# Two-chunk score groups from chunk 10 on, and another order of the first third, in an RWKV-6 layer followed by a squared-ReLU network

## The chip, the core and the metric

The kernel runs on one core of a Trainium2 chip. The metric is device time in microseconds of that core, taken as the median over several executions. One further execution was profiled, and all views of a profile come from that one.

## What is computed

Two parts follow each other. The first is a linear-attention recurrence with a decay for every channel, over 4 batches, 8 heads, 768 steps and a head size of 48. The second is a two-layer network with a squared ReLU on the 3072 tokens of 8 x 48 = 384 features, with 2048 hidden units.

```python
for t in range(S):                       # for every batch and head; state is D x D
    cur = np.einsum('bhd,bhe->bhde', u[None] * kt, vt)
    y[:, :, t] = np.einsum('bhd,bhde->bhe', rt, state + cur)
    state = wt[:, :, :, None] * state + np.einsum('bhd,bhe->bhde', kt, vt)
...
h = x @ w_in          # x: (3072, 384), w_in: (384, 2048)
g = np.maximum(h, 0.0) ** 2
out = g @ w_out       # w_out: (2048, 384)
```

Inputs and outputs are float32. The kernel's matrix products take bfloat16.

## The kernel before

The recurrence is done in chunks of 128 steps: 6 chunks in each of 4 batches, numbered `s` = 0 to 23. Every chunk is a short chain of steps, and each step is a small function that one word of a long string names. For chunk `s` the words are:

- `ld:s:w`, `ld:s:r`, `ld:s:k`, `ld:s:v`: four loads of 192 KB, all issued on SyncE's queue, 192 bytes to a row. Seven buffers of each kind exist.
- `lw` (ScalarE): logarithm of the decay into one of `NLW` buffers. `cum` (TensorE): running sums over the chunk by a triangular matrix, into the two-bank accumulator `cp`; for early chunks (`s < V5`) a second matmul with the negative inclusive triangle; and, for all but a batch's last chunk, five small matmuls with the decay's total.
- `exp` (ScalarE): exponentials of the sums in place, and of the total into `a_c`. For `s >= V5` one sum serves both signs; then `rw` (ScalarE) and `kw` (GpSimd) multiply `k` by the inverse decay first.
- `rd` (VectorE): `r` and `k` times the exponentials. `tr` (TensorE) transposes both, `rkt` (VectorE) copies them out. `p` (TensorE): scores within the chunk, head pairs in halves of 64 rows, into `cp` again. `pm` (VectorE): the mask, from `cp`.
- `su` (TensorE), `ts` (VectorE), `sn` (GpSimd): the state for the next chunk. `ku`, `qp`, `vq` (GpSimd) and `q` (VectorE): the current step's own term with `u`. `v` (ScalarE): `v` in bfloat16.
- `y` (TensorE), `ysb` (VectorE), `yt` (TensorE), `xt` (ScalarE): the output of the chunk, transposed into `xT`.

The network works on blocks of two chunks, `i` = 0 to 11. `m1:i:g:b` is six matmuls of 256 columns into bank `b` of the four banks called `mm`; `rl` (ScalarE) evicts them with the ReLU, `gt` (VectorE) squares. `m2:i:mt:q:b` is four matmuls of 384 columns, a quarter `q` of the sum for one half block; `os` (ScalarE) evicts it and `store` writes it. The weights come as 8 blocks each, `ld:h:I` and `ld:h:O`, 384 KB, and are cast by `cast` on ScalarE or VectorE in turn: `m1` of group `g` needs block I of the same number, `m2` of quarter `q` needs blocks O 2q and 2q+1. `warm` is filler matmuls with no use for the result.

[...] `cp` has two, `y` one, `tr` one (used in turn by `tr`, `su` and `yt`), `mm` four. `cp`, `y`, `tr` and each `mm` bank have one buffer, so the next writer waits until the last reader is done.

The order of the work is written out by hand in the string `order`. Each engine, SyncE's queue included, gets its instructions in the order of the words, and nothing is re-ordered later:

```python
with tc.manual_schedule(engines={E.PE, E.DVE, E.Activation, E.Pool, E.SP}):
    for word in order.split():
        name, *args = word.split(":")
        run[name](*[int(x) if x.isdigit() else x for x in args])
```

## Time and profile before

| what | value |
|---|---|
| median of 6 runs | 199.31 us (198.58 to 200.25) |
| the profiled execution, its own time | 198.89 us |
| its span, first to last instruction | 197.1 us |
| TensorE matmul busy | 188.2 us |
| VectorE, ScalarE, GpSimd busy | 143.9, 131.5, 109.2 us |
| moved from and to memory | 25.17 MB, 4.72 MB |
| `p` on TensorE, 192 matmuls | 9.5 us |
| warm matmuls, 52 recorded | 16.2 us |
| granted TensorE clock | 1.00 |

A chain through all the work of a profile has one slowest engine in each stretch, and the share of a whole span hides which. The profile is therefore read by stages, and a line of the code stands as L with its number. The profiler's span is shorter than the time of the execution by 1.8 us, which lie before the first and after the last instruction.

### The profile page before, as it was taken

What the parts mean: (1) busy time and instruction counts of PE and PEld (TensorE: products, weight loads), DVE (VectorE), ACT (ScalarE), POOL (GpSimd) and SP (SyncE); (2) the same over time, 40 slices, a digit from 0 to 9 for tenths busy, and PEclk for the clock granted to TensorE, in tenths of its full rate; (3) what the DMA queues carried; (4) which work ended last, traced back from release to release, by engine and by line L of the source; (5) the groups of instructions that cost most, each with busy time, mean ns of one, the idle gap of its engine ahead of it and who ended that gap; (6) DMA issues with size and microseconds to landing.
All of it is one profiled execution on the core that took longest, in us unless ns stands there. A gap on an engine that the chain in (4) does not pass through costs nothing.

```text
span 197.1 us, 4956 instructions
## 1 busy us (share of the span) xinstructions
PE 188.2 (95%) x1954; PEld 136.0 (69%) x1958; DVE 143.9 (73%) x202; ACT 131.5 (67%) x278; POOL 109.2 (55%) x124
## 2 busy tenths in 40 slices
PE   7999959999999999999999999999999999999992
PEld 2355546776578777768777688877777778778650
DVE  3369966987788979987969876977897885844210
ACT  3625637895589887878975767678776668438221
POOL 6278643017589899793997299430999390010000
PEclk9999999999999999999999999999999999999999
DMA  6999789989989999899999078605730000015013
GB/s 129 196 212 222 254 233 291 326 216 267 209 177 200 201 203 224 196 196 200 233 200 202 3 171 230 147 16 130 167 68 0 3 0 2 3 40 203 0 40 120
DMA packets 108696, 30.20 MB, mean 153 GB/s; under 512 B 100481, under 2 KB 108674, under 8 KB 108674
## 3 DMA queue, kind: packets, MB, share of 16 engines
q1 hardware_dynamic: 108674, 29.89, 66.0%
q8 instruction: 15, 0.25, 0.5%
q14 instruction: 7, 0.06, 0.1%
HBM read 25.17 MB, written 4.72 MB: 152 GB/s over the span
## 4 chain that ended last, share of the span: by engine, by line
PE 63%; SPq 15%; DMA 8%; DVE 5%; POOL 4%; issue 2%; ACT 2%; DVEq 0%; POOLq 0%; ACTq 0%
PE mm L300 25%; PE mm L324 24%; SPq L67 9%; SPq L90 5%; PE tr L222 4%; DMA w_raw<-in_w_dram 3%; PE cp L234 3%; DMA v_raw<-in_v_dram 3%; DMA rk_raw<-in_r_dram 2%; PE y L269 2%; POOL ku L172 2%; DVE rdec_buf L213 1%; PE tr L285 1%; PE y L274 1%; PE cp L196 1%
## 5 line engine op out<-in xcount | busy, mean ns | idle before, releaser
L300 PE MATMUL mm<-xT,wi_sb 128*128 128x256 bf16 x576 | 72.7, 273 | 2.5 <-ACT wi_sb L104 2.0
L324 PE MATMUL mm<-wo_sb,gt 128*128 128x384 bf16 x384 | 71.6, 326 | 0.0
L309 ACT ACTIVATE rl<-mm 128x512 f16<-128x512 f32 x96 | 55.4, 598 | 18.9 <-PE mm L300 14.1
L300 PEld LDWEIGHTS <-wi_sb 128*128 128x128 bf16 x576 | 54.1, 98 | 12.3 <-ACT wi_sb L104 2.2
L324 PEld LDWEIGHTS <-gt 128*128 128x128 bf16 x384 | 35.8, 98 | 19.0
L317 DVE TENSOR_TENSOR gt<-rl 128x1024 bf16<-128x1024 f16 x48 | 40.2, 854 | 9.5 <-ACT rl L309 9.5
L261 POOL TENSOR_TENSOR S<-t_state,a_c 128x384 bf16<-128x384 f32 x20 | 17.7, 885 | 30.1 <-DVE t_state L257 16.4
L239 DVE TENSOR_TENSOR pmT<-cp,tri_strict 128x1024 bf16<-128x1024 f32 x24 | 29.3, 1219 | 4.3 <-PE cp L234 3.9
L184 POOL TENSOR_TENSOR vq<-v_raw,q 128x384 f32<-128x384 f32 x24 | 21.7, 906 | 17.1 <-DVE q L180 15.4
L172 POOL TENSOR_TENSOR ku<-rk_raw,u_bc 128x384 f32<-128x384 f32 x24 | 25.2, 1048 | 10.5 <-DMA rk_raw<-in_k_dram 5.9
L213 DVE TENSOR_TENSOR rdec_buf<-rk_raw,cp 128x768 bf16<-128x768 f32 x24 | 22.8, 950 | 10.1 <-ACT a_c L209 5.5
L176 POOL TENSOR_TENSOR qprod<-rk_raw,ku 128x384 f32<-128x384 f32 x24 | 25.6, 1074 | 0.6
L226 DVE COPY rkT<-tr 128x1024 bf16<-128x1024 bf16 x24 | 16.5, 687 | 8.4 <-PE tr L222 8.2
L164 POOL TENSOR_TENSOR rk_raw<-rk_raw,rw 128x384 f32<-128x384 f32 x16 | 18.6, 1165 | 5.2 <-ACT rw L160 5.1
L329 ACT ACTIVATE o_sb<-mm 128x384 f32<-128x384 f32 x24 | 11.6, 491 | 9.6 <-PE mm L324 9.5
L288 ACT COPY xT<-tr 128x384 bf16<-128x384 bf16 x24 | 11.5, 479 | 9.6 <-PE tr L285 9.3
L338 PE MATMUL mm<-warm 128*128 128x512 bf16 x52 | 16.2, 427 | 1.5 <-DVE ones L132 1.3
L279 DVE TENSOR_TENSOR y_sb<-vq,y 128x384 bf16<-128x384 f32 x24 | 13.2, 549 | 6.0 <-PE y L274 5.4
L156 ACT ACTIVATE lw_buf<-w_raw 128x384 bf16<-128x384 f32 x24 | 12.4, 521 | 6.3 <-DMA w_raw<-in_w_dram 6.3
L222 PE MATMUL tr<-ident,rdec_buf 128*128 128x128 bf16 x192 | 14.6, 219 | 0.4 <-DVE rdec_buf L213 0.3
L222 PEld LDWEIGHTS <-rdec_buf 128*128 128x128 bf16 x192 | 12.3, 98 | 2.9 <-DVE rdec_buf L213 1.2
L180 DVE TENSOR_REDUCE q<-qprod 128x8 f32<-128x384 f32 x24 | 13.0, 544 | 0.2 <-POOL qprod L176 0.2
(53 smaller groups left out, 178.4 us busy)
## 6 DMA issues: line engine op xcount, KB each, us to landing
w_raw<-in_w_dram SPq DMA_DIRECT2D x24, 192.0 KB, 3.8
rk_raw<-in_r_dram SPq DMA_DIRECT2D x24, 192.0 KB, 3.8
rk_raw<-in_k_dram SPq DMA_DIRECT2D x24, 192.0 KB, 3.9
v_raw<-in_v_dram SPq DMA_DIRECT2D x24, 192.0 KB, 3.8
out_dram<-o_sb SPq DMA_DIRECT2D x24, 192.0 KB, 2.2
...
u_row<-in_u_dram SPq DMA_DIRECT2D x1, 1.5 KB
```

The costliest lines, as they stand in the source:

```text
L67: nc.sync.dma_start(out=dst, in_=src[b, :, c * C:(c + 1) * C, :].rearrange("h c d -> c h d"))
L164: nc.gpsimd.tensor_mul(k_s, k_s, tiles.pop(("rw", s))[:])
L172: nc.gpsimd.tensor_mul(ku[:], raw["rk", s][:, 1], u_bc[:])
L176: nc.gpsimd.tensor_mul(qp[:], raw["rk", s][:, 0], tiles.pop(("ku", s))[:])
L184: nc.gpsimd.tensor_mul(vq[:], raw["v", s][:], tiles.pop(("q", s))[:, :, None].to_broadcast([C, H, D]))
L213: nc.vector.tensor_mul(rdec[:, :, :, 0:D], raw["rk", s][:], tiles.pop(("cs", s))[:, :, 0:DM].rearrange("p a (h d) -> p a h d", h=H))
L222: nc.tensor.transpose(ps_tr[:, i, p, :], rdec[:, i, 2 * p:2 * p + 2, :], ident[:])
L239: nc.vector.tensor_mul(pmT[:].rearrange("p e a t -> p (e a) t"), tiles.pop(("p", s))[:].rearrange("p e (a t) -> p (e a) t", a=HP), tri_str ...
L300: nc.tensor.matmul(ps1[:, j * width:(j + 1) * width], wi_sb[:, kk, n * 128:(n + 1) * 128], xT[:, kk, s0 * C:s0 * C + width], start=(kk == ...
L309: nc.scalar.activation(tiles["rl", i, q][:, j], tiles.pop(("m1", i, g))[:], AF.Relu, scale=RS)
L317: nc.vector.tensor_mul(tiles["gt", i][:, 4 * q:4 * q + 4, :].rearrange("p a b -> p (a b)"), rl, rl)
L324: nc.tensor.matmul(tiles["m2", i, mt][:, 0:DM], gt[:, n, mt * 128:(mt + 1) * 128], wo_sb[:, n, :], start=(n == 0), stop=(n == NT - 1))
```

## The change

Five things differ.

1. From chunk 10 on, `p:s:b0:b1` writes the scores of two chunks with one run of matmuls: chunk `s` into `cp` as before, chunk `s + 1` into two `mm` banks. The second chunk's mask is done by two `pmh`, one for each bank.
2. `V5` goes from 8 to 5, so chunks 5, 6 and 7 take the form with one running sum and get `rw` and `kw`. `NLW` goes from 3 to 4.
3. The five small decay matmuls move from `cum` to `su`, from a `cp` bank to the `tr` bank, and their exponential moves from `exp` to a word of its own, `ac`.
4. The last half block's second layer is done by `last`, in two halves of 192 columns, each with its own eviction (the first on ScalarE, the second on VectorE) and its own store.
5. The order string is another one throughout. In the first third, chunks 4 and 5 are loaded ahead of most weight blocks. `u` is loaded into row 0 of `u_bc`.

The diff, with the order string cut to its first part, the first two-chunk group and the end:

```diff
...
     u_bc = consts.tile([C, H, D], FP32)
-    u_row = consts.tile([1, H, D], FP32)
+    u_row = u_bc[0:1]
     ones_row = consts.tile([1, C], FP32)
     nc.vector.memset(ones_row[:], 1.0)
     def load_u():
-        nc.sync.dma_start(out=u_row[:], in_=u[None])
+        nc.sync.dma_start(out=u_row, in_=u[None])
     def ub_():
         ps = tiles["ub"] = ps_y_pool.tile([C, H, D], FP32, name="y")
-        nc.tensor.matmul(ps[:], ones_row[:], u_row[:], start=True, stop=True)
+        nc.tensor.matmul(ps[:], ones_row[:], u_row, start=True, stop=True)
     def uc_():
         nc.scalar.copy(u_bc[:], tiles.pop("ub")[:])
...
     nc.gpsimd.memset(other_head[:], 0.0)
     nc.gpsimd.memset(other_head[0:DP, :, 1:2], -30000.0)
     nc.gpsimd.memset(other_head[DP:C, :, 0:1], -30000.0)
-    V5 = 8
-    NLW = 3
+    V5 = 5
+    NLW = 4
     lw_bufs = []
     for i in range(NLW):
         t = consts.tile([C, H, DP], BF16, name=f"lw_buf{i}")
...
     def cum_(s):
         lw = tiles["lw", s]
         cs = tiles["cs", s] = ps_cp.tile([C, 2, 512], FP32, name="cp")
-        if s % NCH < NCH - 1:
-            nc.tensor.matmul(cs[:, 0, DM:DM + 2 * HP], ident[:], other_head[:], start=True,
-                             stop=False, skip_group_check=True)
-            for p in range(HP):
-                nc.tensor.matmul(cs[:, 0, DM + 2 * p:DM + 2 * p + 2], lw[:, 2 * p:2 * p + 2, :],
-                                 ones2[:], start=False, stop=True, skip_group_check=True)
         nc.tensor.matmul(cs[:, 0, 0:DM], tri_strict[:], lw[:, :, 0:D], start=True, stop=True)
         if s < V5:
             nc.tensor.matmul(cs[:, 1, 0:DM], tri_incl_neg[:], lw[:, :, 0:D], start=True, stop=True)
...
         else:
             nc.scalar.activation(cs[:, 1, 0:DM], cs[:, 0, 0:DM], AF.Exp, scale=-1.0)
             nc.scalar.activation(cs[:, 0, 0:DM], cs[:, 0, 0:DM], AF.Exp)
-        if s % NCH < NCH - 1:
-            a_c = tiles["a_c", s] = a_small.tile([C, HP, 2], FP32, name="a_c")
-            nc.scalar.activation(a_c[:], cs[:, 0, DM:DM + 2 * HP].rearrange("p (a e) -> p a e", e=2), AF.Exp)
+    def ac_(s):
+        a_c = tiles["a_c", s] = a_small.tile([C, HP, 2], FP32, name="a_c")
+        nc.scalar.activation(a_c[:], tiles["su", s][:, DM:DM + 2 * HP].rearrange("p (a e) -> p a e", e=2), AF.Exp)
     def rd_(s):
         rdec = tiles["rdec", s] = rdec_bufs[s % NRD]
...
         rkT = tiles["rkT", s] = a_mid.tile([C, 2, HP, C], BF16, name="rkT")
         nc.vector.tensor_copy(rkT[:], tiles.pop(("tr", s))[:])
-    def p_(s):
-        rkT = tiles["rkT", s]
-        ps_p = tiles["p", s] = ps_cp.tile([C, 2, 512], FP32, name="cp")
-        for p in range(HP):
+    def p_(s, *banks):
+        tiles["p", s] = ps_cp.tile([C, 2, 512], FP32, name="cp")
+        dst = {s: [tiles["p", s][:, e] for e in range(2)]}
+        if banks:
             for e in range(2):
-                rows = slice(e * DP, (e + 1) * DP)
-                nc.tensor.matmul(ps_p[:, e, p * C:(p + 1) * C], rkT[rows, 1, p, :],
-                                 rkT[rows, 0, p, :], start=True, stop=True)
+                tiles["ph", s + 1, e] = bank(banks[e])
+            dst[s + 1] = [tiles["ph", s + 1, e][:] for e in range(2)]
+        for i in dst:
+            rkT = tiles["rkT", i]
+            for p in range(HP):
+                for e in range(2):
+                    rows = slice(e * DP, (e + 1) * DP)
+                    nc.tensor.matmul(dst[i][e][:, p * C:(p + 1) * C], rkT[rows, 1, p, :],
+                                     rkT[rows, 0, p, :], start=True, stop=True)
     def pm_(s):
         pmT = tiles["pmT", s] = a_mid.tile([C, 2, HP, C], BF16, name="pmT")
...
             tiles.pop(("p", s))[:].rearrange("p e (a t) -> p (e a) t", a=HP),
             tri_strict[:, None, :].to_broadcast([C, 2 * HP, C]))
+    def pmh_(s, e):
+        if ("pmT", s) not in tiles:
+            tiles["pmT", s] = a_mid.tile([C, 2, HP, C], BF16, name="pmT")
+        nc.vector.tensor_mul(
+            tiles["pmT", s][:, e], tiles.pop(("ph", s, e))[:].rearrange("p (a t) -> p a t", a=HP),
+            tri_strict[:, None, :].to_broadcast([C, HP, C]))
+
     def su_(s):
-        rdec, v_bf = tiles["rdec", s], tiles["v", s]
-        ps_su = tiles["su", s] = ps_tr_pool.tile([C, HP, 2, D], FP32, name="tr")
+        rdec, v_bf, lw = tiles["rdec", s], tiles["v", s], tiles["lw", s]
+        ps_su = tiles["su", s] = ps_tr_pool.tile([C, 512], FP32, name="tr")
         for p in range(HP):
-            nc.tensor.matmul(ps_su[:, p], rdec[:, 1, 2 * p:2 * p + 2, :],
+            nc.tensor.matmul(ps_su[:, p * 2 * D:(p + 1) * 2 * D], rdec[:, 1, 2 * p:2 * p + 2, :],
                              v_bf[:, 2 * p:2 * p + 2, :], start=True, stop=True)
+        nc.tensor.matmul(ps_su[:, DM:DM + 2 * HP], ident[:], other_head[:], start=True,
+                         stop=False, skip_group_check=True)
+        for p in range(HP):
+            nc.tensor.matmul(ps_su[:, DM + 2 * p:DM + 2 * p + 2], lw[:, 2 * p:2 * p + 2, :],
+                             ones2[:], start=False, stop=True, skip_group_check=True)
     def ts_(s):
-        ps_su = tiles.pop(("su", s))
+        ps_su = tiles.pop(("su", s))[:, 0:DM].rearrange("p (a e d) -> p a e d", a=HP, e=2)
         ts = tiles["ts", s] = a_mid.tile([C, HP, 2, D], FP32, name="t_state")
         if s % NCH == 0:
-            nc.vector.tensor_copy(ts[:], ps_su[:])
+            nc.vector.tensor_copy(ts[:], ps_su)
         else:
-            nc.vector.tensor_add(ts[:], tiles["S", s][:], ps_su[:])
+            nc.vector.tensor_add(ts[:], tiles["S", s][:], ps_su)
     def sn_(s):
         S = tiles["S", s + 1] = a_mid.tile([C, HP, 2, D], BF16, name="S", bufs=3)
...
         t0 = (blocks[i][0] + mt) * C
         nc.sync.dma_start(out=out[t0:t0 + C, :], in_=tiles.pop(("o", i, mt))[:])
+    def last_(i, mt, b, j):
+        gt, cols = tiles["gt", i], slice(j * DM // 2, (j + 1) * DM // 2)
+        ps, o_sb = bank(b), o_pool.tile([C, DM], FP32, name="o_sb")
+        for n in range(NT):
+            nc.tensor.matmul(ps[:, 0:DM // 2], gt[:, n, mt * 128:(mt + 1) * 128], wo_sb[:, n, cols],
+                             start=(n == 0), stop=(n == NT - 1))
+        if j == 0:
+            nc.scalar.activation(o_sb[:, cols], ps[:, 0:DM // 2], AF.Copy, scale=1.0 / (RS * RS))
+        else:
+            nc.vector.tensor_scalar_mul(o_sb[:, cols], ps[:, 0:DM // 2], 1.0 / (RS * RS))
+        t0 = (blocks[i][0] + mt) * C
+        nc.sync.dma_start(out=out[t0:t0 + C, cols], in_=o_sb[:, cols])
+
     def warm_(n, b):
         ps = bank(b)
         for _ in range(n):
...
-    run = dict(rw=rw_, kw=kw_, lw=lw_, v=v_, cum=cum_, exp=exp_, rd=rd_, tr=tr_, rkt=rkt_, p=p_, pm=pm_, su=su_, ts=ts_,
+    run = dict(rw=rw_, kw=kw_, ac=ac_, last=last_, pmh=pmh_, lw=lw_, v=v_, cum=cum_, exp=exp_, rd=rd_, tr=tr_, rkt=rkt_, p=p_, pm=pm_, su=su_, ts=ts_,
...
-        ld:0:w ld:0:r warm:6:0 ld:1:w ld:0:k lw:0 ld:0:u cum:0 ld:0:v warm:4:1 ld:1:v lw:1 ld:1:r exp:0 ub ld:1:k rd:0
-        warm:1:2 uc ld:2:w cum:1 v:0 ku:0 exp:1 su:0 ld:3:w warm:3:3 ts:0 v:1 tr:0 sn:0 ld:2:v warm:9:0 rd:1 ku:1 ld:2:r
-        rkt:0 qp:0 lw:2 ld:2:k p:0 qp:1 tr:1 pm:0 ld:0:I warm:4:1 ld:3:r ld:4:w rkt:1 cum:2 y:0 exp:2 su:1 ld:3:k
-        warm:10:2 ts:1 v:2 q:1 sn:1 rd:2 ku:2 ld:3:v q:0 cast:i:0:0 p:1 su:2 vq:0 pm:1 warm:5:3 lw:3 ld:1:I ld:2:I qp:2
-        ld:3:I ts:2 cum:3 ld:4:I ysb:0 vq:1 tr:2 exp:3 ld:4:r y:1 rkt:2 ku:3 ld:4:v warm:1:0 rd:3 yt:0 warm:3:1 xt:0
-        qp:3 ysb:1 lw:4 tr:3 sn:2 v:3 p:2 rkt:3 warm:2:2 pm:2 yt:1 ld:5:I warm:4:3 xt:1 cast:i:0:1 cast:i:1:0 p:3 ld:6:I
-        y:2 q:2 m1:0:0:0 pm:3 vq:2 ld:4:k cast:i:2:0 m1:0:2:1 su:3 rl:0:0 ld:5:w ysb:2 m1:0:4:2 ts:3 v:4 cum:4 q:3
-        ld:7:I yt:2 rl:0:4 m1:0:1:3 vq:3 exp:4 y:3 ld:0:O sn:3 warm:3:0 ysb:3 ld:1:O xt:2 cast:i:1:1 rl:0:2 ld:2:O yt:3
-        warm:1:2 ld:3:O m1:0:3:0 xt:3 rd:4 ku:4 ld:6:w cast:i:2:1 m1:1:4:2 ld:4:O qp:4 rl:0:1 su:4 ld:5:k m1:1:5:1 lw:5
-        gt:0:0 m1:0:5:3 rl:0:3 ts:4 rl:1:4 m1:1:2:0 gt:0:1 rl:1:5 m1:1:0:2 cast:i:3:1 rl:0:5 tr:4 cast:i:3:0 rl:1:2
-        m1:1:3:1 rkt:4 ld:5:r cast:o:0:1 m1:0:6:3 gt:0:2 p:4 rl:1:3 m1:1:1:0 cast:o:1:0 rl:1:0 m1:1:6:1 pm:4 rl:1:1
-        ld:5:O m1:1:7:2 cast:o:0:0 ld:6:O gt:1:2 y:4 lw:6 ld:7:O m1:0:7:0 gt:1:0 rl:0:6 cum:5 gt:1:1 rl:0:7 ld:6:k
-        m2:0:0:0:3 exp:5 cast:o:1:1 m2:0:1:0:0 ld:6:r q:4 rl:1:6 m2:0:0:1:3 vq:4 rd:5 cast:o:2:0 m2:0:1:1:0 ld:5:v ku:5
-        m2:1:1:0:1 m2:1:1:1:1 gt:0:3 cast:o:2:1 sn:4 tr:5 cum:6 qp:5 rkt:5 m2:0:1:2:0 exp:6 cast:o:3:0 m2:0:0:2:3 ld:7:w
-        cast:o:3:1 rl:1:7 m2:1:1:2:1 ku:6 q:5 ld:6:v m2:0:0:3:3 rd:6 m2:0:1:3:0 ld:7:k os:0:0 ysb:4 vq:5 tr:6 ld:7:r p:5
-        rkt:6 m2:1:0:0:2 qp:6 lw:7 ld:7:v pm:5 yt:4 v:5 m2:1:0:1:2 os:0:1 ld:8:w xt:4 gt:1:3 cum:7 v:6 y:5 q:6 ld:8:k
-        exp:7 su:6 ysb:5 m2:1:1:3:1 vq:6 ts:6 ld:8:r m2:1:0:2:2 os:1:1 rd:7 sn:6 yt:5 v:7 m2:1:0:3:2 ld:9:k xt:5 ku:7
-        p:6 lw:8 su:7 ld:9:w pm:6 m1:2:6:3 rw:8 qp:7 m1:2:0:0 os:1:0 ld:9:r rl:2:6 ts:7 cum:8 ku:8 y:6 exp:8 tr:7 ld:8:v
-        ysb:6 kw:8 m1:2:7:1 rkt:7 rl:2:0 ld:10:k m1:2:1:2 sn:7 rd:8 rl:2:7 yt:6 m1:2:2:3 ld:10:r ku:9 lw:9 q:7 p:7 xt:6
...
-        rl:11:7 m2:10:0:1:0 rl:11:0 m1:11:1:3 m2:10:1:0:1 rl:11:1 m2:10:0:2:0 gt:11:0 m2:10:0:3:0 gt:11:3 m2:10:1:1:1
-        m1:11:3:2 m2:10:1:2:1 rl:11:3 m2:11:0:0:3 os:10:0 gt:11:1 m2:10:1:3:1 store:10:0 m2:11:1:0:2 m2:11:0:1:3
-        m2:11:0:2:3 m2:11:0:3:3 m2:11:1:1:2 os:11:0 m2:11:1:2:2 os:10:1 store:10:1 m2:11:1:3:2 store:11:0 os:11:1
-        store:11:1
+        ld:0:w ld:0:k warm:6:0 ld:0:r ld:1:w lw:0 ld:0:u cum:0 ld:0:v warm:4:1 ld:1:k exp:0 ld:2:w rd:0 lw:1 tr:0 ld:1:r
+        ub rkt:0 ld:1:v p:0 uc warm:3:2 pm:0 ld:2:v v:0 ku:0 su:0 warm:1:3 ld:2:k ac:0 qp:0 cum:1 y:0 ld:2:r exp:1
+        warm:10:0 ku:1 q:0 ts:0 lw:2 ld:0:I vq:0 rd:1 v:1 ld:3:w qp:1 ld:3:k ysb:0 cum:2 tr:1 exp:2 ku:2 ld:3:r warm:4:1
+        rkt:1 v:2 sn:0 rd:2 yt:0 warm:3:2 xt:0 qp:2 q:1 p:1 ld:4:w su:1 pm:1 warm:5:3 vq:1 ac:1 lw:3 ld:1:I ld:2:I ts:1
+        cum:3 ld:3:v q:2 exp:3 sn:1 tr:2 y:1 rkt:2 ld:5:w warm:2:0 vq:2 ysb:1 su:2 ku:3 warm:5:1 rd:3 ac:2 ld:4:k lw:4
+        cast:i:0:0 qp:3 ts:2 p:2 yt:1 pm:2 warm:2:2 sn:2 xt:1 ld:4:r tr:3 q:3 y:2 v:3 m1:0:0:3 rkt:3 ld:4:v vq:3
+        cast:i:1:0 ysb:2 p:3 ld:3:I lw:5 su:3 cast:i:0:1 ld:5:k warm:1:0 rl:0:0 pm:3 ku:4 m1:0:1:1 ld:4:I ac:3 rw:5
+        warm:2:2 rl:0:1 ld:5:r ts:3 cum:4 y:3 gt:0:0 exp:4 yt:2 warm:4:0 sn:3 ld:5:v ysb:3 xt:2 rd:4 qp:4 v:4 yt:3
+        m1:0:2:3 ld:5:I xt:3 cast:i:1:1 cum:5 rl:0:2 su:4 ku:5 m1:1:0:2 ld:6:w ac:4 exp:5 ts:4 m1:1:1:1 kw:5 q:4 ld:6:k
+        tr:4 rl:1:0 m1:0:3:0 sn:4 rkt:4 cast:i:2:0 ld:6:I m1:1:2:3 rd:5 qp:5 rl:0:3 m1:1:3:2 ld:7:w rl:1:2 gt:0:1 tr:5
+        vq:4 rl:1:1 m1:1:4:0 rkt:5 ld:7:I rl:1:3 cast:i:2:1 p:5 v:5 ld:0:O m1:0:4:3 pm:5 lw:6 ld:1:O m1:1:5:1 ku:6
+        ld:6:r rl:1:4 rw:6 q:5 p:4 rl:1:5 y:5 vq:5 pm:4 ld:2:O m1:0:5:2 cast:i:3:0 ld:3:O kw:6 warm:1:0 ld:4:O ysb:5
+        lw:7 cum:6 ld:6:v warm:1:1 exp:6 gt:1:1 y:4 yt:5 m1:1:6:0 cast:i:3:1 xt:5 m1:0:6:1 rl:0:4 ysb:4 gt:1:0 rl:0:5
+        yt:4 m1:0:7:3 xt:4 gt:0:2 m1:1:7:2 ld:7:k rl:1:6 rl:0:6 m1:2:6:0 rd:6 qp:6 rl:0:7 m1:2:0:1 cast:o:0:1 rl:1:7
+        tr:6 gt:1:2 ld:5:O cast:o:0:0 m1:2:1:3 gt:0:3 cum:7 rl:2:0 m2:1:1:0:2 ld:7:r q:6 rl:2:1 m2:0:1:0:1 cast:o:1:1
+        cast:o:1:0 ld:7:v m2:0:0:0:3 gt:2:0 rw:7 m2:1:1:1:2 gt:1:3 ld:6:O v:6 m2:0:1:1:1 rkt:6 exp:7 ku:7 m2:0:0:1:3
+        ld:7:O su:6 rl:2:6 kw:7 ld:8:w cast:o:2:0 m1:2:7:0 cast:o:2:1 qp:7 ac:6 ld:8:k rd:7 m2:0:1:2:1 v:7 vq:6 ts:6 p:6
+        ld:8:r rl:2:7 q:7 su:7 sn:6 m1:2:2:0 pm:6 ac:7 m2:0:0:2:3 rl:2:2 m2:1:1:2:2 ts:7 cast:o:3:0 ld:9:w cast:o:3:1
+        y:6 tr:7 lw:8 ld:9:k m2:0:1:3:1 rkt:7 rw:8 cum:8 ku:8 m1:2:3:0 ysb:6 ld:8:v exp:8 yt:6 m2:0:0:3:3 kw:8 ld:10:w
+        rl:2:3 m2:1:1:3:2 os:0:0 qp:8 rd:8 ld:11:w m1:2:4:0 lw:9 xt:6 ku:9 q:8 p:7 ld:9:v rl:2:4 m1:2:5:3 pm:7 sn:7 rw:9
...
+        os:2:1 ld:16:w gt:3:2 cum:12 rl:4:0 tr:11 kw:12 m2:3:0:1:2 exp:12 ld:15:k rkt:11 m1:4:4:0 ku:13 ld:14:v rd:12
+        su:10 rl:4:4 m2:3:0:2:2 vq:10 ac:10 ld:16:k p:10:1:3 v:12 ts:10 lw:14 m1:4:2:0 sn:10 pmh:11:1 store:1:1 rw:13
+        su:12 ld:14:r pm:10 rl:4:2 ku:14 m1:4:3:3 store:0:0 m1:4:1:0 ld:15:r rl:4:3 qp:13 q:12 y:10 ld:17:w rw:14
+        pmh:11:0 cum:14 m1:4:5:3 rl:4:1 vq:11 ysb:10 m1:4:6:1 ac:12 lw:15 kw:14 ts:12 ld:16:r m2:3:0:3:2 exp:14 gt:4:0
...
+        gt:10:2 yt:22 m2:9:0:3:0 gt:10:3 xt:22 m2:10:1:2:1 os:9:0 m1:11:2:3 store:9:0 m1:11:3:2 rl:11:2 m1:11:4:0
+        rl:11:3 m1:11:6:3 rl:11:4 m2:10:1:3:1 m1:11:5:2 os:10:1 m1:11:0:0 rl:11:5 m2:10:0:0:1 rl:11:0 gt:11:2 m1:11:1:2
+        gt:11:1 rl:11:6 m2:10:0:1:1 rl:11:1 m2:10:0:2:1 gt:11:0 m1:11:7:0 m2:11:0:0:3 rl:11:7 m2:11:0:1:3 gt:11:3
+        m2:11:0:2:3 m2:11:0:3:3 m2:10:0:3:1 os:10:0 os:11:0 store:10:0 store:10:1 store:11:0 last:11:1:2:0 last:11:1:0:1
```

## The prediction

> **What bounds the kernel now.** I read the engine totals and the slices first, then a table of stages, then the chain of waits with the timeline. The page:
>
> ```profile
> PE 188.2 (95%) x1954; PEld 136.0 (69%) x1958; DVE 143.9 (73%) x202; ACT 131.5 (67%) x278; POOL 109.2 (55%) x124
> ...
> PE   7999959999999999999999999999999999999992
> ...
> DMA  6999789989989999899999078605730000015013
> GB/s 129 196 212 222 254 233 291 326 216 267 209 177 200 201 203 224 196 196 200 233 200 202 3 171 230 147 16 130 167 68 0 3 0 2 3 40 203 0 40 120
> ```
>
> TensorE is busy almost everywhere, and for the first half the DMA engines are too. Busy is not yet useful, since the early matmuls are partly `warm` filler. The stages, cut where the trace changes character:
>
> ```profile
> core 0: us, PE busy (x) PEld busy (x) DVE busy (x) ACT busy (x) POOL busy (x), PEclk, DMA share, GB/s
> 0.00:24.60 24.60, 22.55 (x188) 11.07 (x192) 15.78 (x25) 12.10 (x23) 14.90 (x29) 1.00 0.91 202
> 24.60:34.50 9.90, 7.46 (x89) 5.85 (x86) 6.38 (x10) 5.80 (x11) 4.24 (x5) 1.00 0.99 263
> 34.50:57.30 22.80, 22.34 (x224) 15.59 (x223) 19.21 (x30) 17.22 (x34) 9.34 (x11) 1.00 1.02 248
> 57.30:81.00 23.70, 23.55 (x283) 18.56 (x280) 21.44 (x29) 20.18 (x45) 22.61 (x24) 1.00 1.00 206
> 81.00:193.30 112.30, 112.25 (x1186) 84.89 (x1184) 81.13 (x112) 75.70 (x166) 58.13 (x58) 1.00 0.45 103
> ```
>
> From 81 us on TensorE never rests. So I price TensorE's work and count what is lost. From starts of neighbouring pieces in the chain and the timeline: an `m1` step (6 matmuls) is 0.655 us, an `m2` step (4) 0.65, `tr` 0.445, `yt` 0.17, `su` 0.17, `y` 0.20 plus 0.17 with a state, a `cum` matmul 0.16, the five small decay-sum matmuls 0.13. `p` needs a closer look:
>
> ```profile
> 117.20 0.27 PE L300 MATMUL mm<-xT,wi_sb 128*128 128x256 bf16 x1
> 117.40 0.40 PE L234 MATMUL cp<-rkT 64*128 64x128 bf16 x8
> 117.73 0.39 PE L300 MATMUL mm<-xT,wi_sb 128*128 128x256 bf16 x2
> ```
>
> The last `m1` matmul starts at 117.20; another would follow 0.109 later, but `p` starts 0.20 later: 0.09 lost on entry. From `p` to the next `m1` is 0.33. The eight use 64 rows each, two side by side; if four pairs cost what four 128-column transposes cost (4 x 0.056 = 0.22), 0.11 is lost on leaving. A `p` is thus 0.42, of which 0.20 is switching.
>
> Over all words of the old order (96 `m1`, 96 `m2`, 24 chunks) useful work is 170.0 us. The last matmul ends at 193.3, so 23.3 are lost. The first `m1` of block 2 starts at 57.29 with 35.2 us of useful work ahead of it: **22.1 us are lost before 57.3 and 1.2 after.** Of the first part 56 warm matmuls are 11.9 at 0.213. What holds TensorE there is the loads:
>
> ```profile
> 50.03 0.95 DVE L213 TENSOR_TENSOR rdec_buf<-rk_raw,cp 128x768 bf16<-128x768 f32 x1 [0.85 <-DMA rk_raw<-in_r_dram]
> ...
> 51.04 0.62 PE L222 MATMUL tr<-ident,rdec_buf 128*128 128x128 bf16 x8 [0.31 <-DVE rdec_buf L213]
> ```
>
> Chunk 6's `r` lands at 50.0, `rd:6` follows, then `tr:6`, with TensorE waiting. Landings fit 5.4 us + 0.95 per chunk tensor + 1.25 per weight block up to and with it in SP's order: 50.1 for this one (26 and 16), 27.8 for weight block I4 (seen 27.6), 34.1 for `w` of chunk 5 (seen 34.6). The end is one eviction and a store: the chain has
>
> ```profile
> 186.83 6.51 PE mm L324 x40
> 193.37 0.49 ACT o_sb L329
> ```
>
> and 3.2 us of store until 197.1.
>
> **What the Trainium skill says.** "TensorE: Matmul & The Clock Gate", section "Wait — 56ns, not 53.3ns?", puts a warm matmul at N ÷ 2.4 GHz + about 2.5 ns: 109 ns for 256 columns and 162.5 for 384, which the trace has (0.655/6, 0.65/4); for 192 columns I estimate 82.5 from it. "TensorEngine Tiling (Array Packing)", section "Key Properties": "Changing tiling mode (not just tile) drains the TensorE" — the 0.20 around `p` agrees. "DMA: Bandwidth & Descriptors", section "Specifications", wants 512 B per transfer for full rate; the chunk loads have 192 B rows and run near 200 GB/s here, stretches with weight blocks reach 326.
>
> **The change, part by part**, against the profiled execution (198.89 us, span 197.1; the median of six is 199.31, 0.42 above).
>
> *Two-chunk scores* (`p:10:1:3` and six more): 7 of 24 visits in 64-row mode go, 7 x 0.20 = **-1.40**; the matmuls stay. The second chunk's masking becomes two `pmh` in place of one `pm` of 1219 ns. From 384 columns (549, `y_sb`) and 1024 (1219) follows 1.05 ns per column, so 683 each: 7 x (2 x 683 - 1219) = +1.0 on VectorE, which has 31 idle us after 81; bounds 610 and 683. Two of four `mm` banks are held for one to two us a pair; the `m1` placed next uses a third one and the masking of a bank precedes its next user. Cost 0, bounds -0.5 (a `cp` round trip fewer: at 101.8 `rdec_buf` had waited 1.22 for the exponentials and `a_c`) and +1.5 (0.2 a pair).
>
> *V5 from 8 to 5*: three `tri_incl_neg` matmuls go, 3 x 0.16 = **-0.48**. For chunks 5 to 7 come `rw` (522 ns), two exponentials (484 + 475) for one of 797, and `kw` (1165, or 1.0 undisturbed) on POOL: +2.1 on ScalarE and +3.0 to 3.5 on POOL. POOL is busy 9.3 of 22.8 in that stage, ScalarE 17.2, so both hide; without that cover each `rd` would be some 1 us later.
>
> *Decay sums move from `cum` to `su`, and `a_c` to `ac`*: same 20 x 5 matmuls and 20 x 178 ns; `rd` no longer waits for `a_c`, `sn` now does, and the `tr` bank is held 0.2 longer. 0, bounds -0.2 and +0.4.
>
> *Last tile*: 4 `m2` steps (2.60) become 32 matmuls of 192 columns, 2.64: +0.04. The last eviction is 192 columns on VectorE, 549 - 192 x 1.05 = 350 ns for 491; the half store saves 0 to 0.4. **-0.3**, bounds -0.6 and 0. The other half is evicted and its store issued 1.3 us earlier.
>
> *u in place, fourth `lw_buf`*: one more 0.53 us memset, on POOL before its first wait of 4.5 us; 0.
>
> *The new front.* Warm matmuls are 54 for 56, 0.4 less, but they only fill. Chunks 4 and 5 are loaded earlier, weight blocks later, so the early work is the chunks'. All loads are on SP's one queue; by my fit I7 lands at 41.0, chunk 6's `r` at 44.5, O5 at 51.4, chunk 7's `v` at 53.3, O7 at 55.8. Loss at each gate is landing plus cast or `rd`, less the useful work ahead: `tr:6` 45.5 - 24.0 = 21.5; `su:7` (7v + 0.5) 53.8 - 31.2 = 22.6; the first `m2` of quarter 3 (O7 + a 0.56 cast on VectorE) 56.4 - 34.1 = 22.3, and up to 23.3 as `rd:7`, `ts:6`, `q:7`, `pm:6` and `ts:7` stand ahead on VectorE. Before it was 22.1. I take **+0.5**, bounds 0 and +1.2 from the landings alone. Behind those casts wait `gt` and so all `m2`; behind the `v:7` cast on ScalarE wait the `rl` evictions. A stall earlier than the gates costs nothing while the gates are late: that is its cover.
>
> After the front I keep 1.2 lost, at 0.7 to 2.1. Sum: -1.40 - 0.48 + 0.04 - 0.3 + 0.5 = **-1.6**, that is 197.3 on the profiled time and **197.7** on the median.
>
> **Rivals.** *Fast* (0.52): the sum above, 196.2 to 198.3.
>
> *No change* (0.20): gains eaten. Either O7's cast is at the late bound (+0.6 more) and the held banks cost 0.1 a pair (+0.7), or the second chunk's matmuls of a pair come apart from the first's because their bank is not free, so the array is drained twice as before (+1.4) and the change doesn't do what it says. Both give about 198.9. For it: POOL is busy 22.6 of 23.7 us at 57 to 81, and DMA is at 1.00. Against: from chunk 12 on the loads are far ahead.
>
> *Slower* (0.28): the front loses more than the gates. One mechanism: `rw`, `kw`, `rd` of chunks 5 to 7 are now a chain in series after each `k` landing, 0.5 + 1.0 + 0.95, behind casts and `rl` on ScalarE in a stage where it already works 17.2 of 22.8; `tr:5`, `tr:6`, `tr:7` stand in TensorE's order ahead of `m1` and `m2` that could run. If each is 1.0 late and this adds to the gates, +3.0: about 200.7. It decides from the point where the loss at `cum:8` passes 24.2, the old 22.1 and the 2.1 saved elsewhere. For it: the old order lost 2.0 on one cast there. Against: the work is 2 us for ScalarE's 5.6 idle.
>
> **How the numbers follow.** Half a per cent (1.0 us) is about what a measurement of this kernel can tell from no change. The prediction is the fast case. Its own range is 196.2 to 198.3; both signs are open, so the range runs to 200.7, leaving out the worse half of the slower case; below 196.2 both best bounds would have to hold. The slower case is the largest risk because 22 of the 23 lost us lie in the re-ordered part.
>
> **What would show it.** Right: 17 groups of score matmuls for 24, each pair of 16 taking about 0.55 us to the next matmul; first `m2` of quarter 3 near 57; TensorE without gaps after 81; last matmul near 192.0; a last eviction of 0.35. Wrong: gaps at `tr:5` to `su:7` that bring the loss past 24.2, score groups of 8 after chunk 10, or `m1` waiting on `pmh`.

## The result and the profile after

The changed kernel takes 197.0 us, the median of 35 runs (195.32 to 198.83). The kernel before takes 198.65 us in 70 runs. The ratio is 0.9923, with an interval of 0.9907 to 0.9940: 1.5 us less by the ratio, 1.65 by the medians. The forecast was 1.6 us less; its 197.7 was counted from the 199.31 of six earlier runs. A ratio is of the runs within 1.5% of their kernel's fastest, the median beside it of all runs. The profiled execution took 197.09 us with a span of 195.1, against 198.89 and 197.1.

The same page of the changed kernel, engine totals and slices:

```profile
PE 185.5 (95%) x1965; PEld 136.8 (70%) x1969; DVE 143.5 (74%) x210; ACT 133.3 (68%) x284; POOL 112.6 (58%) x128
...
PE   6899989989999999997999999999999999999993
...
DMA  6999999998999999699999903992210000114004
GB/s 127 201 234 201 241 257 226 273 353 210 303 175 192 178 222 214 149 215 200 222 236 218 225 7 77 211 219 64 91 33 0 3 0 2 44 48 153 3 0 161
```

TensorE is busy for 2.7 us less. Its row of slices shows one thing that the forecast did not have: a 7 in the nineteenth slice, 88 to 93 us, where it had said that there would be no gap. The table of stages, with the same cuts and the same columns as before:

```profile
core 0: us, PE busy (x) PEld busy (x) DVE busy (x) ACT busy (x) POOL busy (x), PEclk, DMA share, GB/s
0.00:24.60 24.60, 21.77 (x194) 11.38 (x198) 17.21 (x28) 11.59 (x22) 16.80 (x32) 1.00 0.93 201
24.60:34.50 9.90, 9.03 (x104) 7.11 (x102) 8.75 (x12) 9.09 (x20) 7.90 (x9) 1.00 1.00 243
34.50:57.30 22.80, 21.64 (x230) 15.82 (x229) 19.14 (x30) 18.66 (x40) 10.18 (x11) 1.00 1.04 268
57.30:81.00 23.70, 23.03 (x248) 16.90 (x246) 19.79 (x26) 19.72 (x46) 19.35 (x21) 1.00 0.93 189
81.00:192.06 111.06, 110.06 (x1203) 85.61 (x1200) 78.29 (x116) 74.24 (x162) 58.33 (x58) 1.00 0.46 107
```

TensorE's idle time between 57.3 and 81 us is 0.67 us here, 0.15 before. After 81 it is 1.00, for 0.05.

The pairs look as the forecast said. The timeline of TensorE around the first one, chunks 10 and 11 (start, duration, then the group):

```profile
83.03 0.49 PE L336 MATMUL mm<-wo_sb,gt 128*128 128x384 bf16 x2
83.45 0.40 PE L234 MATMUL cp<-rkT 64*128 64x128 bf16 x8
83.68 0.39 PE L234 MATMUL mm<-rkT 64*128 64x128 bf16 x8
84.00 0.83 PE L312 MATMUL mm<-xT,wi_sb 128*128 128x256 bf16 x6
```

From the start of the pair at 83.45 to the next `m1` at 84.00 it is 0.55 us, in all seven pairs. A chunk alone takes 0.33 from its start to the next matmul where nothing waits, so the second eight matmuls add 0.22. If the first eight cost the same, 0.11 of the 0.33 is for leaving, as the prediction had reckoned from transposes. The entry comes on top. The masks are, from the groups by form:

```profile
L239 DVE TENSOR_TENSOR pmT<-cp,tri_strict 128x1024 bf16<-128x1024 f32 x17 | 20.7, 1219 | 1.6 <-PE cp L234 1.3
L247 DVE TENSOR_TENSOR pmT<-mm,tri_strict 128x512 bf16<-128x512 f32 x14 | 9.5, 684 | 1.8 <-PE mm L234 1.8
```

684 ns is what the line through 384 and 1024 columns gave (683).

The end of the chain, `last` in its 32 matmuls (2.65 us, where the sum had 2.64), and from the timeline its second eviction:

```profile
186.17 3.25 PE mm L336 x20
189.42 2.65 PE mm L351 x32
```

```profile
192.10 0.36 DVE L356 TENSOR_SCALAR o_sb<-mm 128x192 f32<-128x192 f32 x1 [4.57 <-PE mm L351]
```

The last matmul ends at 192.06, where 192.0 was forecast, and the last eviction takes 0.36 us, where 0.35 was. For the last matmul the agreement is partly luck: two further profiles of the same kernel, below, have 190.65 and 189.39. One sign of the forecast failed: the first `m2` of quarter 3 (`m2:0:1:3:1`) starts at 55.36, not near 57.

### The profile page after: what moved, and what is told of

The parts are those of the page before. It is cut to its first block, busy times and chain, and to the rows that moved or that the text cites. A ratio compares the mean times of both kernels' runs of the same rounds, so it can differ in the third digit from the quotient of the medians.

```text
span 195.1 us, 4992 instructions
## 1 busy us (share of the span) xinstructions
PE 185.5 (95%) x1965; PEld 136.8 (70%) x1969; DVE 143.5 (74%) x210; ACT 133.3 (68%) x284; POOL 112.6 (58%) x128
## 4 chain that ended last, share of the span: by engine, by line
PE 61%; SPq 10%; ACT 7%; DMA 6%; POOL 6%; DVE 4%; issue 3%; DVEq 0%; POOLq 0%; ACTq 0%
PE mm L336 24%; PE mm L312 23%; SPq L67 8%; DMA rk_raw<-in_r_dram 4%; PE tr L216 3%; ACT rl L321 3%; DMA w_raw<-in_w_dram 2%; PE y L281 2%; PE tr L297 2%; POOL qprod L176 2%; SPq L90 2%; PE cp L234 2%; ACT wo_sb L104 2%; POOL ku L172 1%; DVE rdec_buf L207 1%
## 5 line engine op out<-in xcount | busy, mean ns | idle before, releaser
L312 PE MATMUL mm<-xT,wi_sb 128*128 128x256 bf16 x576 | 74.0, 273 | 0.7 <-ACT wi_sb L104 0.7
L321 ACT ACTIVATE rl<-mm 128x512 f16<-128x512 f32 x96 | 55.7, 599 | 20.5 <-PE mm L312 17.1
L336 PE MATMUL mm<-wo_sb,gt 128*128 128x384 bf16 x368 | 69.6, 326 | 0.1
L329 DVE TENSOR_TENSOR gt<-rl 128x1024 bf16<-128x1024 f16 x48 | 39.1, 829 | 12.3 <-ACT rl L321 12.2
L336 PEld LDWEIGHTS <-gt 128*128 128x128 bf16 x368 | 34.5, 98 | 19.0 <-issue 1.4
L172 POOL TENSOR_TENSOR ku<-rk_raw,u_bc 128x384 f32<-128x384 f32 x24 | 26.4, 1101 | 15.2 <-DMA rk_raw<-in_k_dram 10.4
L184 POOL TENSOR_TENSOR vq<-v_raw,q 128x384 f32<-128x384 f32 x24 | 22.4, 937 | 9.4 <-DVE q L180 6.8
L239 DVE TENSOR_TENSOR pmT<-cp,tri_strict 128x1024 bf16<-128x1024 f32 x17 | 20.7, 1219 | 1.6 <-PE cp L234 1.3
L164 POOL TENSOR_TENSOR rk_raw<-rk_raw,rw 128x384 f32<-128x384 f32 x19 | 19.6, 1033 | 1.1 <-ACT rw L160 0.7
L363 PE MATMUL mm<-warm 128*128 128x512 bf16 x50 | 15.3, 421 | 1.5 <-DVE warm L129 1.3
## 6 DMA issues: line engine op xcount, KB each, us to landing
w_raw<-in_w_dram SPq DMA_DIRECT2D x24, 192.0 KB, 4.0
rk_raw<-in_k_dram SPq DMA_DIRECT2D x24, 192.0 KB, 3.9
rk_raw<-in_r_dram SPq DMA_DIRECT2D x24, 192.0 KB, 3.9
v_raw<-in_v_dram SPq DMA_DIRECT2D x24, 192.0 KB, 3.9
out_dram<-o_sb SPq DMA_DIRECT2D x23, 192.0 KB, 2.4
```

The costliest lines, as they stand in the source:

```text
L164: nc.gpsimd.tensor_mul(k_s, k_s, tiles.pop(("rw", s))[:])
L172: nc.gpsimd.tensor_mul(ku[:], raw["rk", s][:, 1], u_bc[:])
L184: nc.gpsimd.tensor_mul(vq[:], raw["v", s][:], tiles.pop(("q", s))[:, :, None].to_broadcast([C, H, D]))
L239: nc.vector.tensor_mul(pmT[:].rearrange("p e a t -> p (e a) t"), tiles.pop(("p", s))[:].rearrange("p e (a t) -> p (e a) t", a=HP), tri_str ...
L312: nc.tensor.matmul(ps1[:, j * width:(j + 1) * width], wi_sb[:, kk, n * 128:(n + 1) * 128], xT[:, kk, s0 * C:s0 * C + width], start=(kk == ...
L321: nc.scalar.activation(tiles["rl", i, q][:, j], tiles.pop(("m1", i, g))[:], AF.Relu, scale=RS)
```

## The experiments

Times are given as a ratio to the kernel before with its interval. "Loss" is used as in the prediction: the start of a piece less the useful TensorE work ahead of it in the order, by the prediction's prices. A pair counts 0.64 in it, and the two matmuls of `ub`, which the list of prices leaves out, 0.55.

### The pair taken apart

The second chunk's scores, still into two `mm` banks, are placed after the next 128-row piece of the order. Seven words become fourteen:

```diff
-  p:10:1:3 v:12 ts:10 lw:14 m1:4:2:0 sn:10 pmh:11:1
+  p:10 v:12 ts:10 lw:14 m1:4:2:0 p:11:1:3 sn:10 pmh:11:1
```

> The changed kernel, but in each of the seven two-chunk groups the second chunk's scores come after the next piece of 128-row work, so that TensorE goes into 64-row mode 24 times and not 17. Theory (each visit costs 0.20 us of switching, 0.09 in and 0.11 out): 7 x 0.20 = 1.4 us of TensorE work more, so the gain over the kernel before shrinks from 1.65 us to about 0.3 (ratio near 0.998), and the trace shows 24 groups of 8 score matmuls with 0.33 us to the next matmul. Rival (the switch isn't what was saved; the gain of the groups is the cp bank being used less often): the ratio stays near 0.992, since the banks are used as in the changed kernel.

Measured: 198.33 us, ratio 0.9982 (0.9952 to 1.0012). Of the change's gain of 0.77% only 0.18% is left: 0.0059 x 198.65 = 1.2 us went with the pairs (about 0.5 to 1.9 by the two intervals), for 1.40 in the sum. The timeline of TensorE around the same two chunks:

```profile
82.49 0.40 PE L235 MATMUL cp<-rkT 64*128 64x128 bf16 x8
82.82 0.83 PE L313 MATMUL mm<-xT,wi_sb 128*128 128x256 bf16 x6
83.58 0.40 PE L235 MATMUL mm<-rkT 64*128 64x128 bf16 x8
83.91 0.34 PE L256 MATMUL tr<-v_bf,rdec_buf 128*128 128x96 bf16 x4
```

Now each of the two has its own 0.33 behind it. The six `m1` between take 83.58 - 82.82 = 0.76, where six with `m1` behind them take 0.655: the entry again. Matmuls, banks and masks are those of the changed kernel, so the switch is what the pairs save. The rival, with a ratio near 0.992, lies outside the interval. One thing spoils the purity: later scores let one `m1` wait for a mask, 0.41 us once at 84.77.

### The last tile alone

The kernel before, with `last` in place of the last four `m2` steps.

```diff
-  m2:11:1:0:2 ... m2:11:1:1:2 ... m2:11:1:2:2 ... m2:11:1:3:2 store:11:0 os:11:1 store:11:1
+  ... store:11:0 last:11:1:2:0 last:11:1:0:1
```

> The kernel before with the last half block's second layer in two halves of 192 columns and nothing else changed. Prediction's term: the stretch from the last matmul's end to the span's end goes from 3.8 us to 3.5, 0.3 faster. Reading of the changed kernel's trace: that stretch is 3.0, so 0.7 faster (ratio near 0.9965). Rival (the halves cost TensorE more than 0.04 us, weight loads not keeping up with 192 columns): no gain. Its first two thirds are the order of before, so the landing times of its loads say how much those vary from one execution to the next: if chunk 7's v lands near 55.2 us again, the 1.4 us by which the same bytes came in sooner in the changed kernel belong to the order of the loads.

Measured: 197.72 us, ratio 0.9984 (0.9948 to 1.0021), which alone tells nothing. Its profile does: from the last matmul's end to the end of the span it is 3.50 us, in the kernel before 3.78. With the 1.77 around the span (1.78 before) that is -0.29, for -0.3 - and the useful work is 0.04 longer, as forecast.

### The weights of quarters 2 and 3 not loaded

Quarters are numbered from 0. The loads of O4 to O7 are left out, and their casts take O0 to O3 again, so this kernel's output differs.

```diff
     def load_wo(h):
+        if h > 3:
+            return
...
-        copy(dst, w_st.pop((kind, h))[:])
+        copy(dst, w_st[kind, h % 4 if kind == "o" else h][:])
```

> The changed kernel without the loads of weight blocks O4 to O7; quarters 2 and 3 of the second layer take blocks O0 to O3 again, so the output differs in that part. All instructions on the compute engines stay; 1.57 MB of the 12.58 MB that the front waits for go. Theory (the front is held by the loads): chunk 7's v lands about 2.5 us sooner (two weight blocks ahead of it go), su:7 goes about 1 us sooner until the front's own chain (y:4, loss 20.8) holds, and the end moves by 0.5 to 1.5 us. Rival (the front is held by its chain of engines): su:7 goes within 0.3 us of where it was and the time stays, ratio near 0.992.

Measured: 195.77 us, ratio 0.9873 (0.9834 to 0.9913). The interval touches that of the change, so a gain over the changed kernel isn't shown, and neither expectation for `su:7` was met. The loads came sooner, `r` of chunk 7 at 48.4 for 50.8 us, but `su:7` went at 53.14, 0.7 later than in the first profile of the changed kernel, in an execution that was 0.6 later already at `y:5`. With O4 to O7 gone the loss at `su:7` is still 21.9 us, and it was 21.4 already at `y:4`, 40.8 us into the span. The changed kernel's own profile says the same: 21.3 at `su:7` and 21.3 at the first `m2` of quarter 3. So **O7 was no gate**: the front's loss is made earlier. After 57 us this run lost 0.2 us; the chunk loads behind the weights come 1.57 MB sooner, but that this is the cause isn't shown.

### What stands before and at 40 us

Most of the loss is older still. These two pieces, of the kernel before and of the changed kernel, have 13.03 and 14.94 us of useful work ahead of them, so 21.0 and 18.9 us are lost at 34 us, of 22.1 and 21.3 at 57:

```profile
33.99 1.25 PE L300 MATMUL mm<-xT,wi_sb 128*128 128x256 bf16 x10
```

```profile
33.87 0.61 PE L216 MATMUL tr<-ident,rdec_buf 128*128 128x128 bf16 x8
```

The timeline of the changed kernel at `y:4`, VectorE and TensorE:

```profile
38.69 0.94 DVE L104 CAST wi_sb<-w_st 128x768 bf16<-128x768 f32 x1
39.54 0.55 DVE L291 TENSOR_TENSOR y_sb<-vq,y 128x384 bf16<-128x384 f32 x1
...
38.82 0.32 PE L190 MATMUL cp<-lw_buf,tri_strict 128*128 128x384 bf16 x1
...
40.14 0.36 PE L281 MATMUL y<-v_bf,pmT 128*128 128x48 bf16 x8 [0.78 <-DVE y_sb L291]
```

There is one `y` bank. `y:4` follows `y:5` in the new order, so it needs `ysb:5`, which stands behind the cast of I6 on VectorE; the bracket says that TensorE was idle 0.78 us for it. Loss rises by 1.16 between `cum:6`, at 38.82, and `y:4`; a warm matmul stands between them too. So the cast was put behind `ysb:5`, in a kernel that also has the two loads of `r` early (below):

```diff
-  pm:4 ld:2:O m1:0:5:2 cast:i:3:0 ld:3:O kw:6 warm:1:0 ld:4:O ysb:5 lw:7
+  pm:4 ld:2:O m1:0:5:2 ld:3:O kw:6 warm:1:0 ld:4:O ysb:5 cast:i:3:0 lw:7
```

> The changed kernel with the loads of r for chunks 9 and 14 ahead of the weights of chunks 10 and 15 (as in the run with r early), and with the cast of the input weight I6 on VectorE placed after the eviction of the first y of chunk 5, no longer ahead of it. Theory 1 (the front's loss is set at the first y product of chunk 5, which waits for that eviction behind the cast): the loss at that product falls by 0.5 to 0.9 us, about as much is left at 57 us, and the time falls by about 0.5 us below the run with r early, ratio to the kernel before about 0.983. Rival: the next gate (the product with I6, the tensor 7v or the weight O5) takes the place of this one; the loss at 57 us is within 0.3 us of the run with r early at equal landing of the first set, ratio about 0.985.

Measured: 195.27 us, ratio 0.9838 (0.9790 to 0.9886), which can't be told from the kernel with `r` early alone (0.9854). Its profile, of one execution, shows more. VectorE, then TensorE:

```profile
39.15 0.54 DVE L291 TENSOR_TENSOR y_sb<-vq,y 128x384 bf16<-128x384 f32 x1
39.61 0.95 DVE L104 CAST wi_sb<-w_st 128x768 bf16<-128x768 f32 x1
```

```profile
39.74 0.36 PE L281 MATMUL y<-v_bf,pmT 128*128 128x48 bf16 x8
...
40.61 1.48 PE L312 MATMUL mm<-xT,wi_sb 128*128 128x256 bf16 x12 [0.17 <-DVE wi_sb L104]
42.53 0.34 PE L297 MATMUL tr<-ident,y_sb 128*128 128x128 bf16 x3 [0.44 <-ACT rl L321]
```

The wait at `y:4` is gone: loss rises there by 0.30, for 1.16. But the first `m1` with I6 now waits for the cast, and `yt:4` waits two pieces on. From `cum:6` to 57 us loss grows by 1.52, and in the kernel with `r` early alone by 1.52. The equal hundredths are chance, since the unchanged kernel has 1.66, 1.52 and 1.86. **The rival holds: the next wait took its place.**

### Two sums up to chunk 7 again

`V5` back to 8 in the changed kernel, with `rw` and `kw` of chunks 5 to 7 taken out of the order.

```diff
-    V5 = 5
+    V5 = 8
...
-  rw:5 ... kw:5 ... rw:6 ... kw:6 ... rw:7 ... kw:7
```

> The changed kernel with V5 = 8 and without rw and kw of chunks 5 to 7: three 384-column matmuls more on TensorE, 2.1 us less on ScalarE and 3 us less on POOL in the front. Theory (the front waits for loads, not for ScalarE or POOL, and TensorE's 0.48 us lie in the stretch that waits): within 0.5 us of the changed kernel, ratio to before 0.992 to 0.995. Rival A (ScalarE and POOL set the front): 0.5 to 1.5 us faster than the changed kernel, 0.985 to 0.989. Rival B (TensorE's work counts in full): 0.5 us slower, 0.995. The loads' order is that of the changed kernel, so O7 should land near 53.8 us again.

Measured: 195.75 us, ratio 0.9871 (0.9827 to 0.9914). By the sum it should have been 0.48 us slower than the changed kernel; it is not slower. The theory's ratios lie above the interval, and the measured one falls among rival A's. Its profile shows what becomes of the second of the three matmuls, the one in `cum:6`:

```profile
38.56 0.32 PE L190 MATMUL cp<-lw_buf,tri_strict 128*128 128x384 bf16 x1
38.72 0.32 PE L192 MATMUL cp<-lw_buf,tri_incl_neg 128*128 128x384 bf16 x1
...
39.88 0.36 PE L281 MATMUL y<-v_bf,pmT 128*128 128x48 bf16 x8 [0.62 <-DVE y_sb L291]
```

From `cum:6` to `y:4` it is 1.32 us here and in the changed kernel above, and the wait is 0.62 for 0.78: the 0.16 us of work took the place of 0.16 us of waiting. From `cum:7` to the next `m2` it is 0.42 in both as well. For the matmul in `cum:5` the traces show no such thing. Whether the lower ratio is more than scatter isn't settled: the interval touches that of the change. The same edit made on top of the early loads of `r` (shown below) gave 196.21 us, 0.9886 (0.9854 to 0.9918), by the ratios 0.6 us slower than these loads alone, with intervals that overlap; so between nothing and the full 0.48 the timed runs don't decide. That run was to tell whether the two gains add up, as rival A would have it; they don't:

> Both edits of the last two runs at once on the changed kernel: r of chunks 9 and 14 loaded earlier, and V5 = 8 without rw and kw of chunks 5 to 7. Theory (V5 = 8 was faster only because r of chunk 14 happened to land 2 us sooner there; with that stall gone the 0.48 us of TensorE work stay): no faster than with the early r alone, ratio to before 0.985 to 0.988. Rival (ScalarE and POOL do hold the front back): the two gains add, ratio near 0.980.

### The decay sums back in the sum's bank

In the changed kernel, the five small matmuls go back from `su` to `cum` and the exponential from `ac` to `exp`.

```diff
-  ac:0 ... ac:22
...
     def exp_(s):
...
+        if s % NCH < NCH - 1:
+            ac_(s)
```

> The changed kernel with the five small decay matmuls back in cum and the exponential of the total back in exp, as before; ac words dropped. Prediction's term: 0 (between 0.2 us slower and 0.4 faster than the changed kernel), ratio 0.991 to 0.994. Rival (the move matters: with ac, VectorE's read of the tr bank for t_state comes after ScalarE's read for a_c, seen as 1.7 us of waits in the changed kernel, and without it rd waits for a_c): more than 0.5 us either way.

Measured: 196.6 us, ratio 0.9913 (0.9882 to 0.9943), within the interval of the change itself. The move costs and brings nothing that could be seen, as the sum had it; an effect of half a microsecond could have stayed unseen.

### `r` of chunks 9 and 14 earlier

In the first profile of the changed kernel the gap at 88 to 93 us is this, from the timeline of VectorE and TensorE:

```profile
90.56 0.95 DVE L207 TENSOR_TENSOR rdec_buf<-rk_raw,cp 128x768 bf16<-128x768 f32 x1 [1.58 <-DMA rk_raw<-in_r_dram]
...
91.56 0.32 PE L190 MATMUL cp<-lw_buf,tri_strict 128*128 128x384 bf16 x1 [1.00 <-DVE rdec_buf L207]
```

`r` of chunk 14 landed at 90.4 us; `rd:14` and with it the `cp` bank for `cum:13` waited, and TensorE 1.00 us with them. On SP's queue `ld:14:r` stands behind `store:1:1`, which holds the queue from 85.12 to 86.58. A smaller step of 0.65 stands at `su:9` at 66.0, `r` of chunk 9 having landed at 64.4. So both loads were moved up:

```diff
-  kw:8 ld:10:w ... rw:9 tr:8 ld:9:r v:8 ... q:11 ld:15:w ... su:12 ld:14:r pm:10
+  kw:8 ld:9:r ld:10:w ... rw:9 tr:8 v:8 ... q:11 ld:14:r ld:15:w ... su:12 pm:10
```

> The changed kernel with two loads moved up in SyncE's queue and nothing else: r of chunk 9 ahead of w of chunk 10 (3 loads earlier), r of chunk 14 ahead of w of chunk 15 (8 places earlier). In the changed kernel rdec_buf of chunk 9 started 0.2 us after that r landed, with VectorE idle for 0.9, and of chunk 14 0.1 us after, idle for 1.6; TensorE then stood still before su:9 (0.6) and cum:13 (1.1). Theory (late r loads set these stalls): both gaps go, 1.2 to 1.7 us faster than the changed kernel, ratio to before 0.984 to 0.986. Rival (the next wait, kw on POOL or the exponentials, is right behind): under 0.5 us, ratio above 0.990.

Measured: 195.9 us, ratio 0.9854 (0.9796 to 0.9913). The gap is gone, and only 0.45 us are lost after 57 us, in a profile of the fastest of the six executions. The ratio is the one that the theory named, but its interval overlaps that of the change. With the cast moved as well this is the kernel above at 195.27, whose interval lies wholly below that of the change; what makes it faster isn't shown, as its profile had lost 21.6 us by 57. By the ratio these two are the fastest of all that were run, below both kernels.

### Each kernel profiled again, unchanged

A single execution had carried both accounts, so each kernel was profiled twice more, the kernel before and the changed kernel on different chips.

> The kernel before, unchanged, for a second profile of its front. Theory 1 (the loss at 57 us follows the landing of the first set of loads, which varies between executions): the first set lands anywhere from 53 to 56 us and the loss at 57 us is that landing less 33.0 us, within 0.3. Rival (the changed order of loads itself brings the set in sooner): it lands at 55 us or later, and the loss is about 22.

> The kernel before, unchanged, for a third profile of its front. The same two theories: landing between 53 and 56 us with a loss of landing less 33.0, or landing at 55 us or later and a loss of about 22.

> The changed kernel, unchanged, for a second profile of it. Theory 1 (r of chunks 9 and 14 is asked for too late and TensorE waits for it): about 2 us are lost after 57 us again, with steps at the state product of chunk 9 and at the sum of chunk 13. Rival (the 2.5 us lost after 57 us in the first profile were an accident of that execution): less than 1.5 us are lost there. In the front, the loss at 57 us lies between 19.9 and 22.2 us in both.

> The changed kernel, unchanged, for a third profile of it. The same two theories: about 2 us lost after 57 us, with steps at the state product of chunk 9 and the sum of chunk 13, or less than 1.5 us.

| profile | last weight or chunk tensor of the first 12.58 MB landed | loss at 34 us | loss at 57 us | lost after 57 | after the last matmul, to the execution's end | span |
|---|---|---|---|---|---|---|
| before | 55.2 | 21.0 | 22.1 | 1.1 | 5.56 | 197.1 |
| before, second | 53.8 | 20.4 | 20.6 | 1.5 | 5.56 | 196.0 |
| before, third | 54.9 | 20.1 | 20.8 | 1.6 | 5.58 | 196.4 |
| after | 53.8 | 18.9 | 21.3 | 2.5 | 5.03 | 195.1 |
| after, second | 53.6 | 19.1 | 21.2 | 1.2 | 5.00 | 193.7 |
| after, third | 53.2 | 17.9 | 20.3 | 0.8 | 5.20 | 192.4 |

What is lost after 57 us is counted here to the start of the last piece; to the end of the last matmul, as the prediction counted, it is about 0.15 more. The run with the last tile alone, whose loads come in the order of before, is a fourth profile of the old front: its last tensor landed at 53.6, and 20.7 us were lost at 57.

Three things follow. First, the kernel before does not always lose 22 us in its front: the profile that the prediction was made from was its worst of three. The old order's set can be in by 53.8 us, where the rival had 55 or later, so the new order isn't needed for an early landing. Loss at 57 us less landing was -33.1, -33.2 and -34.1, so the band of 0.3 that was expected held twice and missed once. The executions differ by 0.9 us already at 34 us, before the last of these loads are even asked for, so the last landing isn't shown to set the loss.

Second, `r` of chunk 14 too late was an **accident** of one execution, as the rival had it. In the second profile of the changed kernel the same two instructions stand so:

```profile
88.64 0.94 DVE L207 TENSOR_TENSOR rdec_buf<-rk_raw,cp 128x768 bf16<-128x768 f32 x1
...
90.15 0.33 PE L190 MATMUL cp<-lw_buf,tri_strict 128*128 128x384 bf16 x1
```

No bracket on either: `r` had landed at 87.0, in the third at 86.3. So the story that early `r` gained its 0.7% by this gap falls. What it brings in the mean of many executions isn't settled; it takes away a wait that one of three profiles had.

Third, spans of one kernel differ by up to 2.7 us (195.1 to 192.4), more than the whole change is worth. A profile tells here where time goes; only the many timed runs tell how much.

## Why the prediction was right, step by step

Two quantities hardly move within a kernel: the useful work, which the order fixes, and the time after the last matmul, in the table. Work fell from 169.99 to 168.15, the end from 5.57 to 5.08 us in the mean. They make -1.84 - 0.49 = -2.33, the first by the prediction's own prices. The timed difference is -1.5 (-1.85 to -1.2). What is left over, +0.8 (0.5 to 1.1 from the interval alone), would be what the new order loses more than the old in front and after it, over all timed runs. The prediction had +0.5 there, all of it in front, with the 1.2 after it kept. This remainder is not a measurement: in the mean of the three profiles of each kernel the new order loses 0.2 less than the old, not more. So the sum was right, its largest term is shown, and the front's term is not.

**The pairs** (-1.40): right. 0.55 us from a pair to the next matmul, 17 groups of scores, 1.2 us lost again when the pairs are taken apart. The Trainium skill's "TensorEngine Tiling (Array Packing)", section "Key Properties", states that a change of tiling mode drains TensorE, without a price; this case's price is 0.20 us for a visit, 0.09 in and 0.11 out, once for a pair. The banks held did no harm: with 684 ns a half, no `m1` of the changed kernel waits for a mask, and one of the kernel taken apart does, for 0.41 us.

**V5** (-0.48): the useful work fell by that; that the time did isn't shown. The step that failed is counting it beside the front's term. The three matmuls stand in the front, where TensorE waits anyway. They had been put in the sum as a gain, and the front's +0.5 was reckoned with the shorter work ahead of its gates, so the total was right. But the two terms are one: -0.48 + 0.5 = 0 for the part up to 57 us. The run with two sums again shows it for two of the three matmuls, whose work stands where the changed kernel waits (0.62 for 0.78 at `y:4`).

**Decay sums** (0): right within what could be seen, 0.9913 against 0.9923.

**The last tile** (+0.04 and -0.3): right for the kernel before with this edit alone, -0.29. In the changed kernel it is -0.49, inside the bounds. The further 0.2 isn't explained by a run.

**The front** (+0.5): the mechanism was wrong, and that the number fitted into a right sum is luck. The gates named were `su:7` by `v` of chunk 7 at 53.3 and quarter 3 by O7 at 55.8. They landed at 51.5 and 53.8, two microseconds ahead of the fit, which was 0.6 late for the last landing even in the execution that it came from (55.8 for 55.2), the slowest of three. Reckoned with these landings the same gates would have given a loss of 52.0 - 31.2 = 20.8 and 54.4 - 34.1 = 20.3, no more than was already lost at 40 us (20.8). The reading of before went the same way: the late `r` of chunk 6 at 50 us, shown as what holds TensorE, added 0.5 to a loss that was 21.0 at 34 us. By 34 us, ahead of every gate named, the changed kernel has lost 18.6 us in the mean and the kernel before 20.5; from there to 57 us it loses 2.3 more and the kernel before 0.7. So the new order gains some 2 us at the start, which the prediction didn't have, and gives most of it back; 1.2 of that at `y:4`, behind the cast of I6 and `ysb:5` on VectorE, with a second wait of like length behind it. What holds TensorE in the first 34 us wasn't tested by a run and stays open. In the three profiles of each, the mean loss at 57 us is 21.2 before and 20.9 after, with executions up to 1.5 apart, so they can't confirm the +0.5, nor its sign.

**The rest** (1.2 lost after the front): 2.5, 1.2 and 0.8, in the mean 1.5; before 1.1, 1.5 and 1.6, in the mean 1.4. The size was right, the statement that there would be no gap after 81 was wrong for one execution in three.

**The rival of a slower kernel** did not come about. The chain `rw`, `kw`, `rd` of chunks 5 to 7 was to show as a loss past 24.2 at `cum:8`; it was 21.3 at most in the three profiles. Whether the chain hides in full, as the sum said, isn't settled: taking it out gave 0.9871, which could be a gain over the change's 0.9923, but on top of the early `r` it gave none.
